# Moving elementwise work between Pool, VectorE and ScalarE in a fused linear-attention and MLP kernel, with a new load order and a scheduler's engine order

## The chip, the cores and the metric

The kernel runs on one core of a Trainium2 chip. The metric is the device time of one execution in microseconds (us).

Engines are named as in the profile: PE is TensorE's matmul, PEld its weight load, DVE is VectorE, ACT is ScalarE, POOL is GpSimd ("Pool"), SP issues the DMAs. L180 means line 180 of that kernel's own file, so the same operation can have another line number in another kernel.

## The reference

```python
# r, k, v: (4, 8, 768, 48); w, u: (8, 48)
def _attn_ref(r, k, v, w, u):
    for t in range(S):
        cur = u*k_t (outer) v_t                    # the diagonal term
        y[:, :, t] = r_t @ (state + cur)
        state = w * state + k_t (outer) v_t
# then x = y as (3072, 384), moe_w_in (384, 2048), moe_w_out (2048, 384)
def _moe_ref(x, w_in, w_out):
    h = x @ w_in
    g = where(h >= 1, h, where(h <= -1, 0, (h + 1)**2 / 4))
    return g @ w_out
```

The listing above is shortened and partly written as formulas. The recurrence over 768 steps is cut into chunks of 128 steps, so that there are 24 units (4 batches x 6 chunks), and each unit is a handful of small matmuls with elementwise work around them. Two units make one block of 256 tokens for the MLP. There are 12 blocks, each with eight steps of `layer1` (h = x @ w_in) and eight of `layer2` (g @ w_out).

The kernel computes `(h + 1)**2 / 4` for every h. That is right only where |h| < 1, so it also computes a bound on |h| from row norms of x and column norms of w_in, and repeats the MLP with the full function if the bound fails. The column norms are the "norms" below.

## The kernel before

The parts that the change touches. Cuts are marked with `# ...`.

```python
    man.enter_context(tc.manual_schedule())      # each engine runs its work in the order written
    # ... loads: four units, then w_in in quarters with two more units between, then w_out
    load()
    u_bc = ...                                    # row broadcast of u
    for _ in range(3):
        load()
    # ...
    def prep(i):                                  # one unit's inputs
        K, R, Vf = loaded.pop(i)
        Rw, Kw = RWp[i % NR], KWi[i % NR]
        nc.gpsimd.tensor_mul(Kw[:, :, 0:D], K, Winv)
        nc.vector.tensor_mul(Rw[:, :, 0:D], R, Wpow)
        V = work.tile([128, H, D], BF16, name="V", tag="V")
        nc.scalar.copy(V, Vf)
        KU = work.tile([128, H, D], F32, name="KU", tag="KU")
        nc.vector.tensor_mul(KU, K, u3)
        nc.gpsimd.tensor_mul(KU, KU, R)
    def s_tr(i):                                  # PE transposes Kw, Rw; ACT evicts them
        # ...
        nc.vector.reduce_sum(diag, KU, axis=mybir.AxisListType.X)
        nc.gpsimd.tensor_mul(VD, V, diag[:, :, None].to_broadcast([128, H, D]))
    # s_at: PE multiplies, VectorE masks
    def s_y(i):                                   # PE: y (output of the chunk) and st (state)
        # ...
        nc.vector.tensor_add(x.rearrange("q (h d) -> q h d", h=H), VD, y)
        if c < NCH - 1:
            if c > 0:
                nc.gpsimd.tensor_mul(X[b], X[b], wc3)
            # ... VectorE adds both halves of st to X[b]
            for s in range(2):
                rows = slice(s * DP, s * DP + D)
                nc.gpsimd.tensor_mul(Tbd[b][rows, :, s * D : (s + 1) * D], X[b][rows], wc3[rows])
    # s_xp: PE transposes x for the MLP, ACT evicts
    def w_norms():
        for q in range(NQ):                       # four quarters of w_in
            # ...
            nc.gpsimd.tensor_mul(sq, wq, wq)
            yield
            nc.gpsimd.tensor_add(sq[:, 0, :], sq[:, 0, :], sq[:, 1, :])
            yield
            nc.gpsimd.tensor_add(sb, sq[:, 0, :], sq[:, 2, :])
            # ... PE sums over partitions, VectorE takes the maximum
    # ...
    for g in range(G0, NB * nP):                  # one MLP step at a time
        m, n = divmod(g, nP)
        layer1(m, n)
        for s, i in plan.get(g, ()):              # stages of later units in between
            stages[s](i)
        layer2(m - 1, n)
        if 6 * nP <= g:
            next(norms, None)
```

In these names K, R and V are one unit's tiles and `wc` is the decay over one chunk. `KWi` and `RWp` are K and R scaled by powers of the decay. `KU` is the product K*u*R, and `diag` is its sum over each head. X (T in the new kernel) is the running state, and `Tbd` is the state in the layout that PE reads. `h_p` and `o_p` are the results of `layer1` and `layer2` in PSUM, `gT` is the activation's output, and `xT` is the transposed x.

## Time and profile before

| | before |
|---|---|
| time, median of 3 runs | 216.61 us (215.42 to 216.70) |
| span of the profiled run | 215.5 us |
| PE busy | 176.2 us |
| PE idle, 0 to 20 us | 13.6 us |
| PE idle, 20 to 60 us | 6.7 us |
| PE idle, 60 to 200 us | 12.7 us |
| PE idle, 200 us to the end | 6.3 us |

The profiled execution itself took 217.31 us.

The first lines are from the page of the kernel before. Part 1 gives busy time, share of the span and number of instructions of each engine. Part 2 has one digit for each fortieth of the span (5.4 us), in tenths busy, with the granted PE clock below. Part 4 shares out the chain of waits that ended last. Part 5 has groups of instructions: busy us, mean ns of one, then the engine's idle time before them and its main releaser.

```profile
PE 176.2 (82%) x1773; PEld 128.2 (59%) x1773; DVE 130.9 (61%) x228; ACT 123.1 (57%) x243; POOL 126.9 (59%) x158
...
PE   0164798799898898999999979747986999999980
...
POOL 6476844725227959288399799799989326000000
PEclk9999999999999999999999999999996999999999
...
PE 38%; POOL 31%; DVE 10%; issue 9%; ACT 5%; SPq 2%; DMA 2%; POOLq 0%; DVEq 0%; ACTq 0%
...
L180 POOL TENSOR_TENSOR KU<-KU,R 128x384 f32<-128x384 f32 x24 | 26.3, 1097 | 16.0 <-DVE KU L179 16.0
...
L179 DVE TENSOR_TENSOR KU<-K,u_bc 128x384 f32<-128x384 f32 x24 | 22.9, 953 | 1.2 <-DMA u_bc<-in_u_dram 1.2
L195 POOL TENSOR_TENSOR VD<-V,diag 128x384 f32<-128x384 bf16 x24 | 19.9, 840 | 5.8 <-DVE diag L193 5.6
...
L307 POOL TENSOR_TENSOR sq<-w_in_sb 128x1536 f32<-128x1536 bf16 x4 | 11.2, 2794 | 0.1
```

POOL is busy for 59% of the span, a modest share, but the chain of waits gives it 31%. The rows of digits show why: where POOL reads 9 for several slices running, past the middle, PE falls to 7 and 4. An average over the span hides that.

The windows view says how much. Its columns are the window, its length, then the busy us of PE, PEld, DVE, ACT and POOL (instructions in brackets), the mean granted PE clock, the DMA share and GB/s.

```profile
0.00:20.00 20.00, 6.40 (x72) 4.71 (x72) 12.56 (x29) 9.14 (x14) 11.95 (x28) 1.00 0.88 198
20.00:40.00 20.00, 16.07 (x164) 12.58 (x161) 16.20 (x31) 14.22 (x30) 12.64 (x16) 1.00 0.90 258
40.00:60.00 20.00, 17.25 (x158) 12.93 (x157) 11.55 (x21) 15.07 (x30) 9.17 (x12) 1.00 0.84 186
60.00:80.00 20.00, 18.23 (x221) 13.22 (x219) 15.17 (x28) 11.30 (x24) 12.01 (x19) 1.00 0.96 209
80.00:120.00 40.00, 38.72 (x416) 28.59 (x414) 29.22 (x46) 25.60 (x52) 30.46 (x34) 1.00 0.50 110
120.00:160.00 40.00, 33.10 (x349) 23.52 (x347) 26.54 (x43) 21.50 (x45) 36.40 (x39) 1.00 0.26 60
```

From 120 to 160 us POOL is busy for 36.4 of 40 us and PE loses 6.9 us. The waits of PE from 60 to 200 us (total us, how often, longest) name the tile:

```profile
PE tr L187 <- POOL KWi_174 L174: 3.4, 2, 2.4
PE tr L187 <- POOL KWi_182 L174: 2.7, 1, 2.7
PE tr L187 <- POOL KWi_186 L174: 2.4, 3, 1.5
PE tr L187 <- POOL KWi_178 L174: 1.7, 3, 0.8
```

Together 10.2 of the 12.7 us. The timeline of the kernel before shows the longest but one (start us, duration us, engine, line, what; the wait and its releaser in brackets):

```profile
160.16 0.82 PE L269 MATMUL h_p<-xT_212,w_in_sb 128*128 128x256 bf16 x6
...
160.57 1.46 POOL L311 TENSOR_TENSOR sb<-sq 128x512 bf16<-128x512 f32 x1
...
162.00 1.30 POOL L174 TENSOR_TENSOR KWi_174<-K,Winv 128x384 bf16<-128x384 f32 x1
...
163.35 0.40 PE L187 MATMUL tr<-ident,KWi_174 128*128 128x128 bf16 x4 [2.37 <-POOL KWi_174 L174]
...
163.89 1.49 PE L287 MATMUL o_p<-w_out_sb,gT 128*128 128x384 bf16 x4
```

POOL works on the norms (`sb`), then on the next unit's `KWi`, and PE waits for it.

### The profile page before, as it was taken

To read this page: it belongs to the slowest core of one execution; us is meant where nothing else is said; L and a number is where in the kernel's file an instruction comes from. 1 tells how busy PE (TensorE), PEld (TensorE's weight loads), DVE (VectorE), ACT (ScalarE), POOL (GpSimd) and SP (SyncE) were. 2 spreads that over 40 slices of the span, in tenths; PEclk is the share of its full clock that TensorE was granted. 3 is DMA by queue.
4 is the path that set the end of the run, shared out by engine and by line. 5 is a ranking of instruction groups with operands and counts; after the bars stand their busy time and mean duration, and the time that the engine had idled before them with its cause. 6 is when DMAs were issued, how large, how long until landed. Compare 5 with 4: busy or idle time off the path is not lost.

```text
span 215.5 us, 4626 instructions
## 1 busy us (share of the span) xinstructions
PE 176.2 (82%) x1773; PEld 128.2 (59%) x1773; DVE 130.9 (61%) x228; ACT 123.1 (57%) x243; POOL 126.9 (59%) x158
## 2 busy tenths in 40 slices
PE   0164798799898898999999979747986999999980
PEld 0143576577566576786776746534663777777650
DVE  4289996784258787686695485693867462611100
ACT  4452769697636768377395574266273559374500
POOL 6476844725227959288399799799989326000000
PEclk9999999999999999999999999999996999999999
DMA  5999889489899962914908508502001001002022
GB/s 98 202 205 328 228 212 341 149 221 207 165 215 223 236 132 73 199 23 111 184 1 191 104 10 183 104 0 78 0 3 42 31 3 68 8 0 75 0 79 84
DMA packets 82781, 25.94 MB, mean 120 GB/s; under 512 B 75840, under 2 KB 81216, under 8 KB 82752
## 3 DMA queue, kind: packets, MB, share of 16 engines
q1 hardware_dynamic: 82752, 25.57, 49.5%
q8 instruction: 16, 0.26, 0.5%
q14 instruction: 13, 0.11, 0.2%
HBM read 20.84 MB, written 4.72 MB: 119 GB/s over the span
## 4 chain that ended last, share of the span: by engine, by line
PE 38%; POOL 31%; DVE 10%; issue 9%; ACT 5%; SPq 2%; DMA 2%; POOLq 0%; DVEq 0%; ACTq 0%
PE o_p L287 16%; PE h_p L269 14%; POOL KU L180 6%; POOL sq L307 5%; POOL sq L309 2%; DMA R<-in_r_dram 2%; POOL Tbd_202 L247 2%; POOL Tbd_199 L247 2%; POOL VD L195 2%; POOL sb L311 2%; POOL KWi_178 L174 2%; POOL Tbd_196 L247 2%; POOL KWi_174 L174 2%; ACT gT L275 1%; PE tr L187 1%
## 5 line engine op out<-in xcount | busy, mean ns | idle before, releaser
L275 ACT ACTIVATE gT<-h_p 128x512 bf16<-128x512 f32 x96 | 57.4, 602 | 52.4 <-PE h_p L269 52.0
L287 PE MATMUL o_p<-w_out_sb,gT 128*128 128x384 bf16 x384 | 77.8, 328 | 1.6 <-ACT o_sb L294 1.6
L269 PEld LDWEIGHTS <-w_in_sb 128*128 128x128 bf16 x576 | 56.5, 99 | 22.1 <-issue 4.6
L287 PEld LDWEIGHTS <-gT 128*128 128x128 bf16 x384 | 34.0, 98 | 18.2 <-issue 2.5
L180 POOL TENSOR_TENSOR KU<-KU,R 128x384 f32<-128x384 f32 x24 | 26.3, 1097 | 16.0 <-DVE KU L179 16.0
L191 ACT COPY RK<-tr 128x1024 bf16<-128x1024 bf16 x24 | 24.4, 1021 | 14.9 <-PE tr L189 14.6
L179 DVE TENSOR_TENSOR KU<-K,u_bc 128x384 f32<-128x384 f32 x24 | 22.9, 953 | 1.2 <-DMA u_bc<-in_u_dram 1.2
L195 POOL TENSOR_TENSOR VD<-V,diag 128x384 f32<-128x384 bf16 x24 | 19.9, 840 | 5.8 <-DVE diag L193 5.6
L292 DVE COPY o_sb<-o_p 128x384 f32<-128x384 f32 x12 | 6.7, 557 | 21.5 <-PE o_p L287 19.7
L193 DVE TENSOR_REDUCE diag<-KU 128x8 f32<-128x384 f32 x24 | 13.0, 547 | 10.3 <-POOL KU L180 10.2
L234 DVE TENSOR_TENSOR x<-VD,y 128x384 bf16<-128x384 f32 x24 | 13.3, 553 | 9.3 <-PE y L224 9.1
L177 ACT CAST V<-V 128x384 bf16<-128x384 f32 x24 | 12.3, 514 | 3.7 <-DMA V<-in_v_dram 3.7
L187 PE MATMUL tr<-ident,KWi_174 128*128 128x128 bf16 x24 | 2.6, 235 | 12.1 <-POOL KWi_174 L174 12.1
L307 POOL TENSOR_TENSOR sq<-w_in_sb 128x1536 f32<-128x1536 bf16 x4 | 11.2, 2794 | 0.1
L247 POOL TENSOR_TENSOR Tbd_199<-X_190,wc 48x192 bf16<-48x192 f32 x10 | 5.0, 504 | 9.3 <-DVE X_190 L242 8.9
L254 PE MATMUL xp<-ident,x 128*128 128x128 bf16 x72 | 8.6, 234 | 1.9 <-DVE x L234 1.9
L205 PEld LDWEIGHTS <-RK 48*128 48x128 bf16 x192 | 6.0, 99 | 6.7 <-issue 4.1
L247 POOL TENSOR_TENSOR Tbd_193<-X_188,wc 48x192 bf16<-48x192 f32 x10 | 5.0, 503 | 8.1 <-DVE X_188 L242 6.7
L269 PE MATMUL h_p<-xT_204,w_in_sb 128*128 128x256 bf16 x48 | 7.6, 308 | 2.3 <-DVE w_in_sb L340 1.5
L187 PEld LDWEIGHTS <-KWi_174 128*128 128x128 bf16 x24 | 1.7, 103 | 12.7 <-POOL KWi_174 L174 12.6
L174 POOL TENSOR_TENSOR KWi_174<-K,Winv 128x384 bf16<-128x384 f32 x6 | 7.0, 1158 | 3.8 <-ACT wc L140 3.5
L175 DVE TENSOR_TENSOR RWp_184<-R,Wpow 128x384 bf16<-128x384 f32 x6 | 8.0, 1340 | 1.5 <-DMA R<-in_r_dram 1.5
(364 smaller groups left out, 362.8 us busy)
## 6 DMA issues: line engine op xcount, KB each, us to landing
K<-in_k_dram SPq DMA_DIRECT2D x24, 192.0 KB, 3.8
R<-in_r_dram SPq DMA_DIRECT2D x24, 192.0 KB, 4.0
V<-in_v_dram SPq DMA_DIRECT2D x24, 192.0 KB, 4.0
out_dram<-o_sb SPq DMA_DIRECT2D x24, 192.0 KB, 2.1
w_in_f<-in_moe_w_in_dram SPq DMA_DIRECT2D x4, 768.0 KB, 6.3
w_out_f<-in_moe_w_out_dram SPq DMA_DIRECT2D x4, 768.0 KB, 5.5
w_bc<-in_w_dram SPq DMA_DIRECT2D x1, 192.0 KB, 3.7
u_bc<-in_u_dram SPq DMA_DIRECT2D x1, 192.0 KB, 4.1
```

The costliest lines, as they stand in the source:

```text
L174: nc.gpsimd.tensor_mul(Kw[:, :, 0:D], K, Winv)
L179: nc.vector.tensor_mul(KU, K, u3)
L180: nc.gpsimd.tensor_mul(KU, KU, R)
L191: nc.scalar.copy(RK, tr)
L193: nc.vector.reduce_sum(diag, KU, axis=mybir.AxisListType.X)
L195: nc.gpsimd.tensor_mul(VD, V, diag[:, :, None].to_broadcast([128, H, D]))
L234: nc.vector.tensor_add(x.rearrange("q (h d) -> q h d", h=H), VD, y)
L247: nc.gpsimd.tensor_mul(Tbd[b][rows, :, s * D : (s + 1) * D], X[b][rows], wc3[rows])
L269: mm(h_p[:, f, :], w_in_sb[:, kk, (2 * n + f) * 128 : (2 * n + f + 1) * 128], xT[m][:, kk, :], start=(kk == 0), stop=(kk == nKb - 1),)
L275: nc.scalar.activation(g, h_p, AF.Square, bias=0.5, scale=0.5)
L287: mm(o_ps[m][j], gT[m][:, f, j * C : (j + 1) * C], w_out_sb[:, f, :], start=(f == 0), stop=(f == nN - 1))
L307: nc.gpsimd.tensor_mul(sq, wq, wq)
```

## The change

The intent is to put each elementwise operation on the engine that has room, and to fill PE's gaps. POOL keeps the products of two SBUF operands. The diagonal term, which needed a product on POOL (VD), is folded into the eight-piece computation of x on VectorE. The decayed state is kept already multiplied (T in place of X), so that Tbd is a cast, which goes to ScalarE. The norms go to ScalarE's Square, with PE doing the sum in one-column matmuls. The loads start w_in two units earlier. The order of the start is rewritten, ScalarE and VectorE exchange the halves of `o_p` that they evict, and the order of each engine is taken from a scheduler that simulates a timeline in place of the order written.

The diff, cut to its core:

```diff
-    man.enter_context(tc.manual_schedule())
+    man.enter_context(tc.block(schedule_with_timeline_sim=True))
 # ... loads: after u, one unit instead of three; then one unit after every quarter of w_in
-    for _ in range(3):
-        load()
+    load()
 # ... prep
-        nc.vector.tensor_mul(Rw[:, :, 0:D], R, Wpow)
+        (nc.vector if i < 6 else nc.gpsimd).tensor_mul(Rw[:, :, 0:D], R, Wpow)
-        nc.scalar.copy(V, Vf)
-        nc.vector.tensor_mul(KU, K, u3)
+        nc.gpsimd.tensor_mul(KU, K, u3)
         nc.gpsimd.tensor_mul(KU, KU, R)
+        if i < 8:
+            nc.scalar.copy(V, Vf)
+        else:
+            nc.gpsimd.tensor_copy(V, Vf)
 # ... s_tr; the reduce_sum of diag moves to s_at
-        nc.gpsimd.tensor_mul(VD, V, diag[:, :, None].to_broadcast([128, H, D]))
 # ... s_y
-        nc.vector.tensor_add(x.rearrange("q (h d) -> q h d", h=H), VD, y)
+        for h in range(H):
+            nc.vector.scalar_tensor_tensor(
+                x[:, h * D : (h + 1) * D], V[:, h, :], diag[:, h : h + 1], y[:, h, :], op0=ALU.mult, op1=ALU.add
+            )
-                nc.gpsimd.tensor_mul(X[b], X[b], wc3)
 # ... VectorE adds st to T[b] instead of X[b]
+            nc.gpsimd.tensor_mul(T[b], T[b], wc3)
-                nc.gpsimd.tensor_mul(Tbd[b][rows, :, s * D : (s + 1) * D], X[b][rows], wc3[rows])
+                nc.scalar.copy(Tbd[b][rows, :, s * D : (s + 1) * D], T[b][rows])
 # ... w_norms: four quarters with three POOL operations each become eight groups
-            nc.gpsimd.tensor_mul(sq, wq, wq)
-            nc.gpsimd.tensor_add(sq[:, 0, :], sq[:, 0, :], sq[:, 1, :])
-            nc.gpsimd.tensor_add(sb, sq[:, 0, :], sq[:, 2, :])
-            mm(n_p, ones, sb, start=True, stop=True)
+            nc.scalar.activation(sq, w_in_sb[:, :, n * 128 : (n + 2) * 128], AF.Square)
+            for f in range(2):
+                for kk in range(nKb):
+                    mm(n_p[:, f : f + 1], sq[:, kk, f * 128 : (f + 1) * 128], ones, ...)
 # ... the start and the plan of the units' stages in a new order (some 100 lines)
-        if 6 * nP <= g:
+        if 5 * nP <= g:
             next(norms, None)
```

More of the change, by code (lines that the diff above doesn't have):

```diff
@@ L108 @@
         w_in_f.append(t)
-        if q in (1, 2):
-            load()
+        load()
     for q in range(NQ):
@@ L153 @@
             lst.append(t)
-    X = [const.tile([128, NP, D], F32, name=f"X{b}") for b in range(B)]
+    T = [const.tile([128, NP, D], F32, name=f"T{b}") for b in range(B)]
     Tbd = []
     for b in range(B):
-        nc.gpsimd.memset(X[b], 0.0)
+        nc.gpsimd.memset(T[b], 0.0)
         t = const.tile([128, NP, 2 * D], BF16, name=f"Tbd{b}")
@@ L174, in prep @@
         nc.gpsimd.tensor_mul(Kw[:, :, 0:D], K, Winv)
-        nc.vector.tensor_mul(Rw[:, :, 0:D], R, Wpow)
+        (nc.vector if i < 6 else nc.gpsimd).tensor_mul(Rw[:, :, 0:D], R, Wpow)
+        KU = work.tile([128, H, D], F32, name="KU", tag="KU")
+        nc.gpsimd.tensor_mul(KU, K, u3)
+        nc.gpsimd.tensor_mul(KU, KU, R)
         V = work.tile([128, H, D], BF16, name="V", tag="V")
-        nc.scalar.copy(V, Vf)
-        KU = work.tile([128, H, D], F32, name="KU", tag="KU")
-        nc.vector.tensor_mul(KU, K, u3)
-        nc.gpsimd.tensor_mul(KU, KU, R)
+        if i < 8:
+            nc.scalar.copy(V, Vf)
+        else:
+            nc.gpsimd.tensor_copy(V, Vf)
         ut[i] = [Rw, Kw, V, KU]
@@ L191, in s_tr @@
         nc.scalar.copy(RK, tr)
-        diag = work.tile([128, H], F32, name="diag", tag="diag")
-        nc.vector.reduce_sum(diag, KU, axis=mybir.AxisListType.X)
-        VD = work.tile([128, H, D], F32, name="VD", tag="VD")
-        nc.gpsimd.tensor_mul(VD, V, diag[:, :, None].to_broadcast([128, H, D]))
-        ut[i] = [Kw, V, RK, VD]
+        ut[i] = [Kw, V, RK, KU]
     def s_at(i):
-        Kw, V, RK, VD = ut[i]
+        Kw, V, RK, KU = ut[i]
         RT, KT = RK[:, 0:NP, :], RK[:, NP : 2 * NP, :]
@@ L210, in s_at @@
             AT.append(a)
+        diag = work.tile([128, H], F32, name="diag", tag="diag")
+        nc.vector.reduce_sum(diag, KU, axis=mybir.AxisListType.X)
         load()
-        ut[i] = [Kw, V, RT, AT, VD]
+        ut[i] = [Kw, V, RT, AT, diag]
     def s_y(i):
         b, c = units[i]
-        Kw, V, RT, AT, VD = ut[i]
+        Kw, V, RT, AT, diag = ut[i]
         y = ps_a.tile([128, H, D], F32, name="y", tag="a")
@@ L233, in s_y @@
         x = work.tile([128, H * D], BF16, name="x", tag="x")
-        nc.vector.tensor_add(x.rearrange("q (h d) -> q h d", h=H), VD, y)
+        for h in range(H):
+            nc.vector.scalar_tensor_tensor(
+                x[:, h * D : (h + 1) * D], V[:, h, :], diag[:, h : h + 1], y[:, h, :], op0=ALU.mult, op1=ALU.add
+            )
         if c < NCH - 1:
-            if c > 0:
-                nc.gpsimd.tensor_mul(X[b], X[b], wc3)
             for s in range(2):
@@ L241, in s_y @@
                 if c > 0:
-                    nc.vector.tensor_add(X[b][rows], X[b][rows], part)
+                    nc.vector.tensor_add(T[b][rows], T[b][rows], part)
                 else:
-                    nc.vector.tensor_copy(X[b][rows], part)
+                    nc.vector.tensor_copy(T[b][rows], part)
+            nc.gpsimd.tensor_mul(T[b], T[b], wc3)
             for s in range(2):
                 rows = slice(s * DP, s * DP + D)
-                nc.gpsimd.tensor_mul(Tbd[b][rows, :, s * D : (s + 1) * D], X[b][rows], wc3[rows])
+                nc.scalar.copy(Tbd[b][rows, :, s * D : (s + 1) * D], T[b][rows])
         ut[i] = x
@@ L290, in layer2 @@
                 o_sb = ewp.tile([128, d_out], F32, name="o_sb", tag="o_sb")
-                if j % 2:
-                    nc.vector.tensor_copy(o_sb, o_ps[m][j])
-                else:
-                    nc.scalar.copy(o_sb, o_ps[m][j])
+                (nc.scalar.copy if j else nc.vector.tensor_copy)(o_sb, o_ps[m][j])
                 b, c = units[m * UB + j]
@@ L297, in layer2 @@
                 nc.sync.dma_start(out=out[t0 : t0 + C, :], in_=o_sb)
-    wn = const.tile([1, NQ], F32, name="wn")
+    wsq = const.tile([128, nN], F32, name="wsq")
     def w_norms():
-        for q in range(NQ):
-            sq = ewp.tile([128, nKb, FQ], F32, name="sq", tag="sq", bufs=1)
-            sb = ewp.tile([128, FQ], BF16, name="sb", tag="sb", bufs=1)
-            wq = w_in_sb[:, :, q * FQ : (q + 1) * FQ]
-            nc.gpsimd.tensor_mul(sq, wq, wq)
-            yield
-            nc.gpsimd.tensor_add(sq[:, 0, :], sq[:, 0, :], sq[:, 1, :])
-            yield
-            nc.gpsimd.tensor_add(sb, sq[:, 0, :], sq[:, 2, :])
+        for n in range(0, nN, 2):
+            sq = ewp.tile([128, nKb, 256], BF16, name="sq", tag="sq", bufs=2)
+            nc.scalar.activation(sq, w_in_sb[:, :, n * 128 : (n + 2) * 128], AF.Square)
             yield
             yield
-            yield
-            n_p = ps_a.tile([1, FQ], F32, name="n_p", tag="a")
-            mm(n_p, ones, sb, start=True, stop=True)
-            nc.vector.reduce_max(wn[:, q : q + 1], n_p, axis=mybir.AxisListType.X)
+            n_p = ps_a.tile([128, 2], F32, name="n_p", tag="a")
+            for f in range(2):
+                for kk in range(nKb):
+                    mm(
+                        n_p[:, f : f + 1], sq[:, kk, f * 128 : (f + 1) * 128], ones,
+                        start=(kk == 0), stop=(kk == nKb - 1),
+                    )
+            nc.vector.tensor_copy(wsq[:, n : n + 2], n_p)
             yield
@@ L322, in bound_fails @@
         nc.gpsimd.tensor_copy(identf, ident)
-        xm = const.tile([128, 1], F32, name="xm")
-        nc.vector.reduce_max(xm, xn, axis=mybir.AxisListType.X)
-        x_p = ps_a.tile([1, 128], F32, name="x_p", tag="a")
-        nc.tensor.transpose(x_p, xm, identf)
+        xm = const.tile([128, 2], F32, name="xm")
+        nc.vector.reduce_max(xm[:, 0:1], xn, axis=mybir.AxisListType.X)
+        nc.vector.reduce_max(xm[:, 1:2], wsq, axis=mybir.AxisListType.X)
+        x_p = ps_a.tile([1, 2, 128], F32, name="x_p", tag="a")
+        for i in range(2):
+            nc.tensor.transpose(x_p[:, i, :], xm[:, i : i + 1], identf)
         m2 = const.tile([1, 2], F32, name="m2")
-        nc.vector.reduce_max(m2[:, 0:1], x_p, axis=mybir.AxisListType.X)
-        nc.vector.reduce_max(m2[:, 1:2], wn, axis=mybir.AxisListType.X)
+        nc.vector.reduce_max(m2, x_p, axis=mybir.AxisListType.X)
         flag = const.tile([1, 1], mybir.dt.int32, name="flag")
@@ L346, in cast_out, with each @@
             eng(w_out_sb[:, f : f + TQ // 2, :], w_out_f[q][:, i * (TQ // 2) : (i + 1) * (TQ // 2), :])
+    def each(m, ns, layer):
+        for n in ns:
+            layer(m, n)
     prep(0)
@@ L350 @@
     s_tr(0)
+    s_at(0)
     s_tr(1)
-    s_at(0)
+    cast_in(0)
+    s_y(0)
+    s_at(1)
     prep(2)
-    s_at(1)
-    s_y(0)
+    cast_in(1)
+    s_xp(0)
+    s_y(1)
+    cast_in(2)
+    prep(3)
+    s_xp(1)
+    each(0, (0, 1), layer1)
     s_tr(2)
-    prep(3)
-    s_y(1)
+    cast_in(3)
+    prep(4)
+    each(0, (2, 3), layer1)
     s_at(2)
-    s_xp(0)
+    cast_out(0)
     s_tr(3)
-    s_xp(1)
+    each(0, (4,), layer1)
     s_y(2)
+    prep(5)
+    cast_out(1)
+    each(0, (5,), layer1)
@@ L364 @@
     s_at(3)
-    cast_in(0)
     s_xp(2)
+    each(0, (6,), layer1)
+    s_tr(4)
     s_y(3)
-    layer1(0, 0)
+    each(0, (7,), layer1)
     s_xp(3)
-    layer1(0, 1)
-    cast_in(1)
-    layer1(1, 0)
-    layer1(1, 1)
-    prep(4)
-    layer1(0, 2)
-    layer1(0, 3)
-    s_tr(4)
-    layer1(1, 2)
-    layer1(1, 3)
-    cast_in(2)
-    s_at(4)
-    prep(5)
-    layer1(0, 4)
-    layer1(0, 5)
-    s_y(4)
-    s_tr(5)
-    layer1(1, 4)
-    layer1(1, 5)
-    cast_in(3)
-    s_at(5)
-    layer1(0, 6)
@@ L392 @@
-    layer1(0, 7)
-    s_y(5)
-    s_xp(4)
-    layer1(1, 6)
-    s_xp(5)
-    layer1(1, 7)
-    cast_out(0)
+    cast_out(2)
+    prep(6)
+    cast_out(3)
+    for n in range(nP):
+        layer1(1, n)
+        if n == 0:
+            s_at(4)
+        elif n == 2:
+            s_y(4)
+        elif n == 3:
+            s_tr(5)
+        elif n == 4:
+            s_xp(4)
+        elif n == 5:
+            s_at(5)
+    prep(7)
+    for n in range(4):
+        layer2(0, n)
+        if n == 0:
+            s_y(5)
+        elif n == 2:
+            s_xp(5)
@@ L399 @@
     for n in range(nP):
         layer1(2, n)
-        if n % 2 == 1 and n < nP - 1:
-            cast_out(n // 2 + 1)
-        if n in (5, 7):
-            prep(6 + n // 7)
-        layer2(0, n)
-    for n in range(nP):
-        layer2(1, n)
-        stages[1 + n // 2](6 + n % 2)
+        if n < 4:
+            layer2(0, 4 + n)
+        else:
+            layer2(1, n - 4)
+        if n == 2:
+            s_tr(6)
+        elif n == 4:
+            s_at(6)
+        elif n == 5:
+            s_tr(7)
+        elif n == 7:
+            s_y(6)
@@ L411 @@
+    s_at(7)
+    layer2(1, 4)
+    s_xp(6)
+    layer2(1, 5)
+    s_y(7)
+    layer2(1, 6)
+    layer2(1, 7)
+    s_xp(7)
     G0 = 3 * nP
     plan = {}
-    for m in range(4, NB):
-        for s in range(5):
-            for j in range(UB):
-                g = m * nP - 11 + 2 * s + j if m > 4 else G0 + s + j
-                plan.setdefault(max(g, G0), []).append((s, m * UB + j))
+    for i in range(4 * UB, len(units)):
+        m, j = divmod(i, UB)
+        g = max(m * nP - 15 + 4 * j, G0 - 5 + 3 * (i - 4 * UB))
+        for s, at in enumerate((0, 2, 4, 7, 9)):
+            plan.setdefault(max(g + at, G0), []).append((s, i))
```

## The prediction

> **What bounds it now.** TensorE, with two leaks. The page gives PE 176.2 us busy (82% of a 215.5 us span), DVE 61%, POOL 59%, ACT 57%. PE idles 39 us; the windows view places it: 13.6 us in the first 20 us, 6.7 us from 20 to 60 (the DMA share is 0.9 to 1.0 from 10 to 30), 12.7 us from 60 to 200, 6 us at the end. In the dense stretch 47.6 to 56.7 one step of the MLP takes 1.31 us, so 96 steps are 126 us, and 24 attention units take about 2.1 us each.
>
> The middle leak is POOL. From 120 to 160 POOL is busy 36.4 of 40 us while PE loses 6.9; the chain of waits runs through KU, KWi, Tbd and sq on POOL there, and the waits view has PE's transposes wait for KWi.
> POOL and VectorE also slow each other. KU*R takes 0.99 us alone and 1.31 us beside a VectorE product; VectorE's K*u takes 0.54 us at best, 0.95 in the mean, 1.35 at worst. The Trainium skill ("GPSIMD Engine Reference", Specifications) says that the SBUF interface is shared and that VectorE instructions with two SBUF inputs contend; this trace agrees.
>
> **What the change does.**
> - POOL loses VD (19.9 us), the norms (21.5) and the Tbd products (21.5); it gains K*u (24 x 1.0), R*Wpow for 18 units (18 x 1.0) and V's cast for 16 (estimate 0.5 each). 127 falls to about 112 us: some 5.2 us a unit, against 7.4 that PE needs.
> - VectorE loses K*u (22.9) and 18 of R*Wpow (about 18). x becomes eight 128x48 instructions: a 48x192 copy takes 0.35 us, so I estimate 0.15 to 0.2 each, 1.2 to 1.6 us a unit instead of 0.55. About 112 to 115 us.
> - ScalarE loses 16 casts (8.2), gains 40 state casts (estimate 0.3 to 0.36) and 8 squares (0.85): 123 to about 135 us. In the norm stretch it is near 13 of each 15 us.
> - PE gains 48 one-column matmuls, loses four of 0.43 us: about +1 us.
> - Loads: w_in's first quarter comes two units earlier, w_out later, behind more units.
> - The scheduler reorders every queue: POOL and loads run units ahead, layer2 fills gaps; VectorE's first weight cast stands ahead of unit 0's x.
>
> **On the critical path.** Middle: of 12.7 us idle I expect 3 to 5 to remain, gain 8 to 9. Start: VectorE is 89 to 96% busy from 10 to 30 and its work for six units is about unchanged, so layer1 starts near 23 instead of 28 us but with fewer units done: gain 2 to 3. End: 0. Against it: +1 PE, +1 ScalarE waits. 215.5 - 3 - 8.5 + 2 = 206 us span.
>
> **Predicted: 206.5 us, 80% range 199 to 213.** Faster by over 2%: 0.84; within: 0.12; slower: 0.04.
>
> **What would show it.** Right: PE idle between 60 and 200 under 6 us; POOL out of the chain there, KU*R near 1.0 us; PE busy 175 to 179; first layer1 at 22 to 25 us. Wrong: DVE instructions of x over 0.25 us each; PE waiting for gT or h_p behind ScalarE's squares; w_out casts holding VectorE at 45 to 60.
>
> **What would make it wrong.** A static order made from modelled durations that blocks in-order queues (VectorE's casts waiting for a DMA); w_out landing later; ScalarE at near 90% delaying the two h_p buffers.

## The result, and the profile after

A ratio is the mean time of one kernel's runs over the mean of the other's runs of the same rounds, so it is not quite the ratio of the medians quoted beside it. Executions over 1.5% slower than the fastest of the same kernel are left out of the means.

| | before | after |
|---|---|---|
| time, median of 4 runs | 216.21 us | 200.06 us (199.80 to 201.24) |
| ratio, 95% interval | | 0.927 (0.922 to 0.932) |
| span of the profiled run | 215.5 us | 197.9 us |
| PE busy | 176.2 us | 173.8 us |
| PE idle, 0 to 20 us | 13.6 us | 13.5 us |
| PE idle, 20 to 60 us | 6.7 us | 4.9 us |
| PE idle, 60 to 200 us (after: to 192.5, where its last matmuls end) | 12.7 us | 0.3 us |
| PE idle, the tail (before: from 200 us; after: from 192.5) | 6.3 us | 5.4 us |

The page of the kernel after, the same parts:

```profile
PE 173.8 (88%) x1818; PEld 129.5 (65%) x1818; DVE 113.0 (57%) x358; ACT 136.0 (69%) x275; POOL 110.3 (56%) x144
...
PE   0263697789999999999999999999999999999990
...
POOL 7498664979797999994667846927513100000000
PEclk9999999999999999999999999999999999999999
...
PE 67%; ACT 5%; DMA 3%; DVE 3%; issue 1%; ACTq 0%
...
L234 DVE SCALAR_TENSOR_TENSOR x<-V,diag,y 128x48 bf16<-128x48 bf16 x192 | 35.9, 258 | 23.7 <-PE y L223 18.9
...
L175 POOL TENSOR_TENSOR KU<-K,u_bc 128x384 f32<-128x384 f32 x24 | 24.5, 1020 | 2.1 <-DVE diag L209 1.8
L176 POOL TENSOR_TENSOR KU<-KU,R 128x384 f32<-128x384 f32 x24 | 24.2, 1011 | 0.8
```

POOL's share of the span has hardly changed, 59% to 56%. It has left the chain of waits altogether, and from the tenth slice on PE reads 9. KU*R takes 1011 ns in the mean where it took 1097. The windows of the kernel after:

```profile
0.00:20.00 20.00, 6.51 (x61) 4.04 (x62) 11.81 (x40) 11.75 (x21) 14.47 (x29) 1.00 0.93 203
20.00:40.00 20.00, 16.09 (x176) 12.10 (x175) 19.46 (x53) 16.32 (x35) 13.58 (x15) 1.00 1.04 232
40.00:60.00 20.00, 18.97 (x222) 15.11 (x222) 13.83 (x45) 18.52 (x41) 17.20 (x22) 1.00 0.95 208
60.00:80.00 20.00, 19.73 (x205) 14.61 (x203) 11.63 (x37) 12.31 (x26) 18.43 (x23) 1.00 1.05 194
80.00:120.00 40.00, 40.00 (x437) 29.50 (x436) 22.97 (x78) 30.21 (x63) 28.52 (x35) 1.00 0.73 157
120.00:160.00 40.00, 40.00 (x439) 30.33 (x438) 23.35 (x75) 28.98 (x61) 18.06 (x24) 1.00 0.09 32
```

From 80 us on PE never idles until the tail. POOL has become early: 18.4 of 20 us from 60 to 80, and only 18.1 of 40 from 120 to 160, where it had 36.4. And of PE's waits from 60 to 200 us, one line is left:

```profile
PE h_p L270 <- ACT xT_206 L257: 0.3, 1, 0.3
```

The difference of the spans, 17.6 us, is the sum of the table's rows: 12.4 us of idle time in the middle, 1.8 from 20 to 60, about 1 at the two ends together, and 2.4 us less of PE busy time. Of that last term, about 1.4 us is an estimate from the mean granted clock (0.991 of 176.2 us against 0.999); the rest I cannot place.

### The profile page after: what moved, and what is told of

Its sections match the earlier page's. It is cut to its first block, busy times and chain, and to the rows that moved or that the text cites. A ratio compares the mean times of both kernels' runs of the same rounds, so it can differ in the third digit from the quotient of the medians.

```text
span 197.9 us, 4831 instructions
## 1 busy us (share of the span) xinstructions
PE 173.8 (88%) x1818; PEld 129.5 (65%) x1818; DVE 113.0 (57%) x358; ACT 136.0 (69%) x275; POOL 110.3 (56%) x144
## 4 chain that ended last, share of the span: by engine, by line
PE 67%; ACT 5%; DMA 3%; DVE 3%; issue 1%; ACTq 0%
PE o_p L288 30%; PE h_p L270 24%; DMA w_out_f<-in_moe_w_out_dram 3%; PE y L223 2%; ACT gT L276 2%; PE tr L190 2%; PE tr L188 2%; PE xp L255 1%; DVE x L234 1%; PE y L220 1%; PE st L231 1%; ACT RK L192 1%; PE n_p L309 1%; ACT w_out_sb L343 0%; DVE T_189 L242 0%
## 5 line engine op out<-in xcount | busy, mean ns | idle before, releaser
L288 PE MATMUL o_p<-w_out_sb,gT 128*128 128x384 bf16 x384 | 73.5, 326 | 0.0
L270 PEld LDWEIGHTS <-w_in_sb 128*128 128x128 bf16 x576 | 53.8, 99 | 12.6 <-issue 1.0
L234 DVE SCALAR_TENSOR_TENSOR x<-V,diag,y 128x48 bf16<-128x48 bf16 x192 | 35.9, 258 | 23.7 <-PE y L223 18.9
L288 PEld LDWEIGHTS <-gT 128*128 128x128 bf16 x384 | 35.8, 98 | 18.4
L175 POOL TENSOR_TENSOR KU<-K,u_bc 128x384 f32<-128x384 f32 x24 | 24.5, 1020 | 2.1 <-DVE diag L209 1.8
L176 POOL TENSOR_TENSOR KU<-KU,R 128x384 f32<-128x384 f32 x24 | 24.2, 1011 | 0.8
L255 PE MATMUL xp<-ident,x 128*128 128x128 bf16 x72 | 10.7, 226 | 2.4 <-DVE x L234 2.3
L181 POOL CAST V<-V 128x384 bf16<-128x384 f32 x16 | 8.1, 504 | 7.2 <-PE h_p L270 4.7
L172 POOL TENSOR_TENSOR KWi_185<-K,Winv 128x384 bf16<-128x384 f32 x6 | 6.0, 998 | 8.2 <-PE st L231 5.2
L172 POOL TENSOR_TENSOR KWi_173<-K,Winv 128x384 bf16<-128x384 f32 x6 | 6.0, 997 | 7.1 <-ACT Winv L137 3.5
L255 PEld LDWEIGHTS <-x 128*128 128x128 bf16 x72 | 6.4, 99 | 4.9 <-DVE x L234 3.6
L172 POOL TENSOR_TENSOR KWi_177<-K,Winv 128x384 bf16<-128x384 f32 x6 | 6.0, 997 | 4.6 <-DMA K<-in_k_dram 3.8
L172 POOL TENSOR_TENSOR KWi_181<-K,Winv 128x384 bf16<-128x384 f32 x6 | 6.8, 1132 | 2.7 <-DMA K<-in_k_dram 1.3
L292 ACT COPY o_sb<-o_p 128x384 f32<-128x384 f32 x12 | 5.7, 477 | 2.8 <-PE o_p L288 2.7
```

Of the source, the lines that this page charges most:

```text
L175: nc.gpsimd.tensor_mul(KU, K, u3)
L234: nc.vector.scalar_tensor_tensor(x[:, h * D : (h + 1) * D], V[:, h, :], diag[:, h : h + 1], y[:, h, :], op0=ALU.mult, op1=ALU.add)
L255: nc.tensor.transpose(xp[:, kk, :], x[:, kk * 128 : (kk + 1) * 128], ident)
L270: mm(h_p[:, f, :], w_in_sb[:, kk, (2 * n + f) * 128 : (2 * n + f + 1) * 128], xT[m][:, kk, :], start=(kk == 0), stop=(kk == nKb - 1),)
L288: mm(o_ps[m][j], gT[m][:, f, j * C : (j + 1) * C], w_out_sb[:, f, :], start=(f == 0), stop=(f == nN - 1))
L292: (nc.scalar.copy if j else nc.vector.tensor_copy)(o_sb, o_ps[m][j])
```

## The experiments

Two theories stood against each other. P, the prediction's: the moved operations relieve POOL, and that is the gain. S: the scheduler's order is the gain, and the moved operations are secondary. All twelve kernels gave correct results, and each was timed against the kernel before on the same chip. In the three batches the kernel before took 216.94 to 216.99 us in the median.

Two cautions hold for the comparisons below. The changed kernel was measured in a batch in which the kernel before took 216.21 us, so a difference between its median and that of an experiment comes out 0.4 to 1.9 us larger than from the ratios. And under the scheduler an edit can change the order of the whole kernel, so each such time is that of an edit together with one new order.

### The changed kernel in the order written

```diff
 (against after)
-    man.enter_context(tc.block(schedule_with_timeline_sim=True))
+    man.enter_context(tc.manual_schedule())
```

> The changed kernel with each engine's order as the source writes it, no scheduler. Theory P (the gain comes from taking work off POOL and ending its contention with VectorE): most of the gain stays, 201 to 205 us, PE idle from 60 us on still under 4 us. Theory S (the scheduler's order gives the gain): 209 us or more, with new waits of PE for ACT, DVE or POOL in the middle.

Measured: 233.03 us, ratio 1.077 (1.071 to 1.083). Without the scheduler the change makes the kernel 16 us slower than before. POOL's timeline in this run shows what happens:

```profile
57.21 1.00 POOL L176 TENSOR_TENSOR KU<-KU,R 128x384 f32<-128x384 f32 x1
63.66 0.51 POOL L245 TENSOR_TENSOR T<-T,wc 128x192 f32<-128x192 f32 x1 [5.45 <-DVE T L242]
80.06 0.51 POOL L245 TENSOR_TENSOR T<-T,wc 128x192 f32<-128x192 f32 x1 [15.90 <-DVE T L242]
84.09 0.51 POOL L245 TENSOR_TENSOR T<-T,wc 128x192 f32<-128x192 f32 x1 [3.52 <-DVE T L242]
84.56 1.00 POOL L172 TENSOR_TENSOR KWi<-K,Winv 128x384 bf16<-128x384 f32 x1
```

`T*wc` of the current unit must wait for VectorE's sum of the state, and VectorE's sum for PE. The products of the next unit stand behind it in POOL's queue, although their inputs are there: `KWi` at 84.56 starts without a wait of its own. The Trainium skill ("Perfetto Trace Analysis", Per-engine timelines) calls the queues of ACT, DVE and GPSIMD strict FIFO, and this trace agrees: POOL stands for 15.9 us before one instruction of 0.51 us. In all POOL waited 60.6 us for these sums of T, in 16 waits, and 15.2 us more, in 4, for T of the first chunks. The scheduler is a necessary part of this change's gain.

### The kernel before with the scheduler only

```diff
 (against before)
-    man.enter_context(tc.manual_schedule())
+    man.enter_context(tc.block(schedule_with_timeline_sim=True))
```

> The kernel before with the scheduler's order and nothing else. Theory P: POOL's work and contention are as before, so 212 to 217 us, with POOL still over 90% busy from 120 to 160. Theory S: 206 us or less.

Measured: 209.31 us, ratio 0.964 (0.961 to 0.968), between the two expectations. One line changed gives 7.7 us, under half of the gain. The windows of this run:

```profile
20.00:80.00 60.00, 49.66 (x490) 37.26 (x486) 51.95 (x87) 41.04 (x83) 56.59 (x64) 0.89 1.02 237
80.00:200.00 120.00, 120.00 (x1204) 88.88 (x1201) 63.62 (x113) 73.00 (x144) 59.79 (x67) 1.00 0.23 60
```

PE is 100% busy from 80 to 200 us with all of POOL's old work still on POOL. So the middle leak needs no removal of work: it closes when POOL runs ahead. The work is then done earlier, and the loss moves with it: from 20 to 80 us POOL is busy 56.6 of 60 us, PE 49.7, at a granted clock of 0.89. In the kernel after, this window has 54.78 us of PE at a clock of 1.00.

### The moved operations without the scheduler, in the old order

```diff
 (against before: prep to s_y, w_norms, bound_fails and the eviction of o_p as in after;
  loads, start, plan and the threshold 6 * nP of the norms as in before; manual_schedule stays)
```

> The kernel before with all the moved operations (products on POOL, diagonal inside x, state cast and norms on ScalarE), but with the old order as written, the old loads and the old plan. Theory P: 204 to 208 us, PE idle from 60 on falls from 12.7 to under 5 us, nothing gained in the first 60 us. Theory S: over 212 us.

Measured: 244.60 us, ratio 1.127 (1.122 to 1.132). P fell here. The moved operations alone lose 28 us, and POOL waits 77.1 us for the sums of T. A likely reason, only argued here, is that the kernel before also has state products on POOL that wait for VectorE's sum, but with K*u and R*Wpow on VectorE far fewer products of the next unit stand behind them.

### Is it only the state product?

If `T*wc` is all that blocks POOL in the order written, taking it off POOL must give the time back.

```diff
 (against the changed kernel in the order written)
-            nc.gpsimd.tensor_mul(T[b], T[b], wc3)
+            nc.vector.tensor_mul(T[b], T[b], wc3)
```

> The changed kernel in the order as written (233 us), with one operation moved: the state's product T*wc on VectorE right behind the state's sum. Theory O (POOL's in-order queue stands before T*wc, 61 us of waits, while products of later units that are ready stand behind it): POOL's waits for the state go, 207 to 218 us. If the loss has another cause: 228 us or more.

Measured: 240.31 us, ratio 1.107 (1.102 to 1.113). That theory fell: it got slower, not faster. The waits for T are gone and others have come in their place. POOL's largest group of waits in this run:

```profile
POOL KU L175 <- DVE diag L209: 32.0, 15, 8.9
```

And POOL's timeline:

```profile
67.29 0.99 POOL L173 TENSOR_TENSOR RWp<-R,Wpow 128x384 bf16<-128x384 f32 x1
77.16 1.00 POOL L175 TENSOR_TENSOR KU<-K,u_bc 128x384 f32<-128x384 f32 x1 [8.87 <-DVE diag L209]
```

K*u now stands for 8.9 us until VectorE's sum over an earlier KU has freed a buffer. The blocking does not come from this one instruction alone: POOL's queue has early and late work of different units, each with a partner on an engine that is itself in order.

### Only the norms moved, nothing else

This takes the prediction's main term by itself: the kernel before, in its order, with ScalarE and PE doing the norms.

```diff
 (against before: wn, w_norms and bound_fails as in after; start of the norms at 6 * nP as in before)
-            nc.gpsimd.tensor_mul(sq, wq, wq)
-            ...
+            nc.scalar.activation(sq, w_in_sb[:, :, n * 128 : (n + 2) * 128], AF.Square)
+            ...
```

> The kernel before, in its order as written, with only the norms moved to ScalarE. The step of the prediction (POOL's work is the middle leak): 208 to 212 us, PE idle between 120 and 160 falls from 6.9 to under 3 us. If order decides and not work: 214 to 219 us.

Measured: 209.04 us, ratio 0.964 (0.960 to 0.969). The window in which the kernel before lost 6.9 us of PE:

```profile
120.00:160.00 40.00, 38.31 (x439) 28.91 (x439) 28.71 (x53) 30.47 (x61) 28.33 (x36) 1.00 0.32 67
```

POOL goes from 36.40 to 28.33 us, PE from 33.10 to 38.31, and PE's waits for KWi between 120 and 166 us are gone. This confirms the mechanism of the prediction in the middle. PE's idle time from 60 to 200 us falls from 12.7 to 5.5 us here, and to 1.5 us in the kernel before under the scheduler, so the norms alone and the scheduler alone, which gain 7.9 and 7.7 us, draw on the same leak. That the two gains cannot be added is argued from this: the two were not run together without the other moves. All moved operations together give 3.1 us more under the scheduler in the old order, as the next runs show.

### Old and new operations, old and new order, all under the scheduler

Two more kernels complete a table of four. One has after's loads, start and plan with before's operations, the other before's loads, start and plan with after's operations.

```diff
 (old operations, new order: after, with prep to s_y, w_norms, bound_fails and the
  eviction of o_p as in before; threshold 5 * nP as in after)
 (new operations, old order: the moved operations without the scheduler, as above, and)
-    man.enter_context(tc.manual_schedule())
+    man.enter_context(tc.block(schedule_with_timeline_sim=True))
```

> The scheduler, the new loads and the new source order, but every operation as before (products on VectorE, VD, state and norms on POOL). Scheduling the kernel before gave 209.3 us; the changed kernel is at 200.1. Theory M (the moved operations give the last 9 us, by relieving VectorE and POOL in the first 80 us): 206 to 211 us, POOL over 90% busy from 20 to 60. Theory L (load order and source order give them): 200 to 203 us.

> The mirror: the scheduler and all moved operations, but the old loads and the old source order. Theory M: 200 to 204 us. Theory L: 207 to 211 us.

Measured: 209.93 us, ratio 0.969 (0.963 to 0.976), for the old operations in the new order, as theory M had it; and 206.19 us, ratio 0.950 (0.945 to 0.955), for the new operations in the old order, between M and L.

| under the scheduler, median us | old operations | new operations |
|---|---|---|
| old loads, start and plan | 209.31 | 206.19 |
| new loads, start and plan | 209.93 | 200.06 |

The moved operations gain 3.1 us in the old order and 9.9 in the new. The new loads and start gain nothing with the old operations and 6.1 us with the new. With the old operations POOL is busy for 39.0 of 40 us between 20 and 60 us, so an earlier start of PE's work finds POOL full. The gain of the whole is more than the sum of its parts here. By the ratios the 9.9 us are 9.3 and the 6.1 us are 5.1. I have not separated the loads from the order of the start.

### The norms put back on POOL

```diff
 (against after: w_norms and bound_fails as in before; threshold 5 * nP as in after)
```

> The changed kernel with the weight norms back on POOL (about 21 us of POOL work). Theory P with the norms as its largest part: PE idle of 3 us or more comes back between 100 and 160, 203 to 206 us. If the norms do not matter once the rest is moved (POOL is 66% busy from 100 to 140 and runs units ahead): 199 to 202 us.

Measured: 209.42 us (207.16 to 209.96), ratio 0.961 (0.955 to 0.968). Both expectations were too low: this one part costs 9 us of the changed kernel's gain, and what is left is only 0.5 us better than the old operations in the new order, which is within the spread of the runs. The windows of this run, and then a line of POOL's timeline:

```profile
20.00:80.00 60.00, 50.89 (x485) 37.58 (x486) 44.46 (x113) 40.42 (x83) 51.45 (x54) 0.91 0.98 227
80.00:200.00 120.00, 119.52 (x1214) 88.52 (x1212) 64.22 (x209) 79.90 (x164) 65.91 (x76) 1.00 0.26 64
```

```profile
17.70 2.75 POOL L305 TENSOR_TENSOR sq<-w_in_sb 128x1536 f32<-128x1536 bf16 x1 [0.43 <-DVE w_in_sb L338]
```

The loss is between 20 and 80 us, and not in the middle at all. It is not idle time alone: this profile is 10.2 us longer than that of the changed kernel, 4.5 us in PE's idle time and 5.7 in its busy time (179.5 against 173.8 us), and the granted clock was 0.50 from 39.0 to 45.8 us and for 3.4 us from 56.1 on. The one execution with a mean clock of 0.995 took 207.16 us, the other three, at 0.971 to 0.979, took 209.40 us or more. The scheduler put the square of the first quarter at 17.7 us, as soon as its weights were there, although the source has it far later. So the next question was whether the place of the norms costs the 9 us or their amount.

### The norms on POOL, held back to the middle

A one-column copy makes the first square depend on a result of unit 9, so that the scheduler cannot draw it forward. The column is overwritten by the square, so the result stays right.

```diff
 (against the run above)
+            if q == 0:
+                nc.vector.tensor_copy(sq[:, 0, 0:1], xn[:, 9:10])
             nc.gpsimd.tensor_mul(sq, wq, wq)
```

> The changed kernel with the norms on POOL (209.4 us when the scheduler put two of the four quarters between 20 and 60 us), now made to depend on unit 9's norm, so that the scheduler cannot put them before about 80 us. Theory of place (the norms cost because they were drawn into the full start of POOL): 199 to 203 us. Theory of work (21 us of POOL work cost wherever they stand): 206 to 210 us.

Measured: 209.11 us, ratio 0.965 (0.961 to 0.970). The theory of the place fell. The windows show the start recovered and the loss moved:

```profile
20.00:80.00 60.00, 54.22 (x588) 41.63 (x589) 43.49 (x133) 46.55 (x98) 50.75 (x59) 1.00 0.97 223
80.00:200.00 120.00, 116.38 (x1127) 85.75 (x1125) 57.32 (x186) 74.57 (x151) 65.87 (x70) 0.97 0.27 69
```

But it does not follow that POOL lacks the time. In the middle of the loss POOL itself idles:

```profile
156.54 1.00 POOL L172 TENSOR_TENSOR KWi<-K,Winv 128x384 bf16<-128x384 f32 x1 [6.36 <-PE st L231]
```

POOL waits here for PE's `st`, which the static order has placed late. My argument, not shown, is that the scheduler chose an order for a POOL that it believed to be full, and that this order exposed a chain of VectorE, PE and ACT which the chip ran differently. What is shown is that norms on POOL cost 9 us by the medians (7.5 and 8.4 by the ratios) under the scheduler in either place; why just so much stays open.

### The products of K and R on VectorE

```diff
 (against after)
-        (nc.vector if i < 6 else nc.gpsimd).tensor_mul(Rw[:, :, 0:D], R, Wpow)
+        nc.vector.tensor_mul(Rw[:, :, 0:D], R, Wpow)
-        nc.gpsimd.tensor_mul(KU, K, u3)
+        nc.vector.tensor_mul(KU, K, u3)
```

> The changed kernel with K*u of every unit and R*Wpow of every unit back on VectorE, nothing else. If the shared SBUF interface matters for the time: POOL's KU*R slows from a mean of 1.01 to 1.1 us or more, VectorE's K*u has a mean near 0.8 us, and the time is 203 to 208 us, lost in the first 60 us. If it only costs engines that have slack under the scheduler: 199 to 202 us with the same slower instructions.

Measured: 203.28 us, ratio 0.938 (0.933 to 0.942). These two moves are worth 3.2 us by the medians and 2.4 by the ratios. The time is in the range of the first expectation, and the loss is before 100 us. The groups of this run:

```profile
L176 POOL TENSOR_TENSOR KU<-KU,R 128x384 f32<-128x384 f32 x24 | 25.9, 1081 | 22.7 <-DVE KU L175 10.6 <-issue 7.1 <-DMA K<-in_k_dram 1.9
...
L175 DVE TENSOR_TENSOR KU<-K,u_bc 128x384 f32<-128x384 f32 x24 | 15.7, 653 | 2.7 <-DMA u_bc<-in_u_dram 1.3 <-DMA K<-in_k_dram 1.1
```

POOL's KU*R slows from 1011 to 1081 ns when VectorE has two-input products again. The slowing that the prediction named is real, but here it is 7% on POOL, and 24 of them make only 1.7 us. Both signs that the expectation set are missed: KU*R stayed under 1.1 us, and K*u under 0.8. So it is not shown that the shared interface costs the time. A rival is VectorE's work itself, which is busy for 52.6 of the 60 us from 20 to 80 us here and for 44.9 in the changed kernel. VectorE's K*u is at 653 ns, not the 953 of before, so much of its slowness in the kernel before probably comes from what ran beside it there; which instruction, I have not tested.

### Two attempts to beat the changed kernel

In the kernel after, VectorE is 97% busy from 20 to 40 us, and the first two squares of the norms run on ScalarE at 16.3 us, in the crowded start. The first attempt holds them back by the same means as above; the second also gives R*Wpow of units 3 to 5 to POOL.

```diff
 (against after, first attempt)
+            if n < 4:
+                nc.vector.tensor_copy(sq[:, 0, 0:1], xn[:, 9:10])
             nc.scalar.activation(sq, w_in_sb[:, :, n * 128 : (n + 2) * 128], AF.Square)
 (second attempt: the same, and)
-        (nc.vector if i < 6 else nc.gpsimd).tensor_mul(Rw[:, :, 0:D], R, Wpow)
+        (nc.vector if i < 3 else nc.gpsimd).tensor_mul(Rw[:, :, 0:D], R, Wpow)
```

> The changed kernel with its two early squares on ScalarE held back behind unit 9's norm (1.6 us of ScalarE at 16 to 18 us freed). Theory of place: 198 to 200 us, at most 1.5 us faster than the changed kernel. If it is only another draw of the scheduler: within 2 us of 200 either way.

> As e14, and R*Wpow moves to POOL from unit 3 on instead of unit 6. VectorE is 97% busy from 20 to 40 us in the changed kernel, POOL 68%; 3 us of products leave VectorE there. If VectorE's sum bounds the start: 196.5 to 199 us. If POOL's latency takes its place: 199 to 203 us.

Measured: 201.36 us (200.79 to 203.53), ratio 0.931 (0.926 to 0.935), and 202.29 us (201.12 to 205.52), ratio 0.931 (0.926 to 0.935). The 205.52 us are an execution 2.2% above the fastest; the other five have a median of 201.73 us and are at most 203.11. Neither attempt beats 200.06 us, and both intervals overlap that of the changed kernel (0.922 to 0.932), so they cannot be called slower either. The theory of place is not confirmed by the first. In the second, VectorE is relieved as meant (97% to 68% busy from 20 to 40 us), and PE then waits for the casts of w_out and POOL is fuller. The start is held by several engines at once.

## Why the prediction was right or wrong

The direction and the range were right: 200.06 us lies in 199 to 213, near its lower end. The centre, 206.5, was 6.4 us too high.

1. "The middle leak is POOL": right. The chain of waits after has no POOL, KU*R is at 1011 ns, and the norms alone, taken off POOL, give 7.9 us, with PE's waits for KWi gone.
2. "Of 12.7 us idle I expect 3 to 5 to remain, gain 8 to 9": the mechanism was right and the term was mis-sized. 0.3 us remained, and the gain was 12.4 us. The estimate counted less work on POOL as fewer waits. The scheduler run of the kernel before shows the second lever: with POOL's work unchanged and only run ahead, PE was 100% busy from 80 to 200 us. After has both.
3. "Start: gain 2 to 3": nearly right. Idle time from 0 to 60 us fell by 1.9 us. By 80 us PE had done 61.3 us of work where it had done 57.9. The first `layer1` matmul came at 23.65 us (predicted 22 to 25) instead of 27.8.
4. "+1 PE, +1 ScalarE waits": wrong in sign. PE busy fell from 176.2 to 173.8 us instead of rising, and PE waited for ScalarE for 0.3 us from 60 to 200. The 48 one-column matmuls are busy for 2.3 us as a group; they start about 25 ns apart, so I estimate that they cost some 1.2 us. Not foreseen was that without gaps the granted clock stays up, which makes up about 1.4 us by the estimate above.
5. Engine totals were right: POOL 110.3 (112 predicted), VectorE 113.0 (112 to 115), ScalarE 136.0 us (135). The pieces of x took 1.49 us a unit (1.2 to 1.6). A single one lasts 258 ns, which is over the 0.25 us that the prediction set as a sign of being wrong. But they start 175 ns apart in the median and overlap, so the group's busy time and not the mean duration is what counts.
6. What the prediction did not see at all is how the parts depend on each other. It named a static order as a risk. In the runs the static order was what made the moved operations as a whole a gain: the moved operations and the new order, left in the order written, take 233.0 us, though the norms alone are a gain of 7.9 us in the old order as written. The prediction counted the moved operations as a gain in themselves, and together they were a loss of 28 us until the scheduler ordered them. That its number held all the same owes something to luck.

The sum: 206 us of span was predicted. The middle gave about 3.9 us more than 8.5, PE's work and ScalarE's waits 4.4 less than the +2, and the tail about 1 us, with the start about 1 us short of 3; that makes 197.9 (206 - 3.9 - 4.4 - 1 + 1.1, rounded).

## What to carry to other kernels

Look for the stretch in which an engine with a modest share of the span is full, and ask first whether its work can run earlier there before asking what work to take away: here both closed the same leak, and all the moves together added only 3.1 us to the scheduler's gain in the old order. A move of work onto an in-order engine is also a change of its queue, so try the moved work with the order that it will run in; here the same moves cost 28 us in the old order as written, and gained 3.1 us in the old and 9.9 us in the new order under the scheduler. When PE's gaps close, the granted clock may rise too: here from 0.991 to 0.999 in the mean of the profiled executions (0.982 to 0.992 in the other runs of the kernel before, 0.994 to 0.996 in those of the kernel after).

## What the Trainium skill lacked or had wrong

- "TensorE: Matmul & The Clock Gate", Part 1, gives an idle window of about 3.4 us as what drops the clock, and matmuls of about double the time then. In the kernel before, one gap of 2.37 us, after 12 us without a gap, was followed by 3.4 us at a clock of 0.50, and four matmuls took 1.49 us instead of 0.81 (1.8 times); the longest gap, of 2.7 us, was not. With the norms back on POOL under the scheduler, the clock was 0.50 from 39.0 to 45.8 us, and no gap of PE from 33 to 39 us was over 0.7 us, but PE was busy for only 3.0 of the 5.5 us before the drop. A look for gaps over 3.4 us alone would have missed both, and no run here shows what the rule is.
- "GPSIMD Engine Reference", Specifications, says that SBUF interfaces are shared with VectorE and that its instructions with two SBUF inputs contend. The runs agree, but that row gives no size, and other pages, which say more about how the two engines block each other, were not tested here. Measured: KU*R took 1011 ns in the mean with few such instructions on VectorE, 1081 with 48 products of 128x384 there, 1097 in the kernel before, and 1.30 us was seen for one product of KWi.
- "VectorE: DVE Perf Modes", the section on the TRN2 errata, has 120 + FD cycles at 0.96 GHz for PSUM to SBUF, an estimate of 175 ns for 48 columns. The piece of x (scalar_tensor_tensor with a column as scalar, one input in PSUM) agrees, if the row is read as the spacing of starts: 175 ns in the median. The duration that the profile shows for one piece is longer, 258 ns, so that neighbours overlap there, and eight take 1.49 us.
- "Perfetto Trace Analysis", Per-engine timelines, says that these queues are strict FIFO. No page that I read says what this costs when work of several units shares a queue: 60.6 us of waits for one product in one kernel here, and 77.1 us in another.
